# A recurrent attention and an MLP on one core: a new order of emission, placed by the program's scheduler instead of by hand

## The chip, the cores and the metric

The kernel runs on one core of a Trainium2 chip. The metric is the device time of one execution, in microseconds (us). PE is the matrix engine (TensorE), DVE the vector engine, ACT the scalar engine, POOL GpSimd and SP the engine that issues most transfers. Each engine takes its own instructions in a fixed order and waits, at the head of its queue, for what the next one needs. Differences within some tenths of a per cent are the spread of a single kernel.

## The reference

```python
def _attn_ref(q, k, v, alpha):          # (4, 8, 768, 48)
    for t in range(S):
        state = alpha[:, :, t, :, None] * state + np.einsum('bhd,bhe->bhde', k[:, :, t], v[:, :, t])
        y[:, :, t] = np.einsum('bhd,bhde->bhe', q[:, :, t], state)

def _moe_ref(x, w_in, w_out, g_ln):     # x: the attention's y as (3072, 384)
    h = x @ w_in                        # d_ff 1024
    e = np.exp(h - h_max)
    solu = h * (e / (np.sum(e, axis=-1, keepdims=True) + 1e-09))
    ln = (solu - mu) / np.sqrt(var + 1e-06) * g_ln
    return (ln @ w_out).astype(np.float32)
```

q, k, v and alpha are fp32. The weights and the gains of the norm arrive as float64; the kernel turns the words of the weights into fp32 itself.

## The kernel before

**Attention in groups.** The 768 tokens are cut into G = 6 groups of 128; a group covers all 4 batches and 8 heads at once. Within a group the recurrence is written as a masked product. Alpha is transposed (`alpha_T`, L165), so that tokens run along a row; a backward scan gives `hT` (`scan_back`, L181, three instructions of a third each), and a forward scan, seeded by a reciprocal from `hT`, gives the decays that belong to the queries, in `aT` (`scan_on`, L186). Keys are transposed and multiplied by `hT` (`keys_T`, `keys`), queries by `aT` (`queries_T`, `queries`). In `queries` POOL multiplies the ends of the heads' 48 columns (`qe`), ACT separates them into two halves of a head pair (`apart`), and POOL multiplies the first 32 columns (`qv`). PE forms scores (`scores`, L233, in two halves of four heads), DVE masks them into `sT` (`masked`). PE then reads the state with the queries (`read_state`, four parts) and the values with the scores (`read_values`) into y; ACT copies y as four tiles `xT`, one for each batch. `next_state` multiplies the keys turned back (`keys_back`, `kg`) by the values into kv, and DVE adds kv to `state`, which `decay` has scaled on POOL.

**MLP in blocks.** A block n is 128 tokens of one batch, 24 in all, four to each group. `up(n, half)` makes one half of h on PE, then e on ACT, u on DVE and its square on ACT; `partial(n)` adds up e on POOL and the squares on DVE; `down(n, half)` multiplies u by w_out, its second half also forms the two sums; `finish(n)` takes the sums on DVE, a power on POOL, and scales the output on ACT (`o_sb`), which SP writes out.

**Weights.** `pieces` are six parts of w_in (512 wide) and eight of w_out (384 wide). For each: `fetch` loads the raw words on SP's queue into one of four buffers, `bits` makes two fp32 parts by four DVE operations (L437 to L444), `add` sums them on PE (L457) and copies the sum by ACT, `in_range` runs two ACT operations over the raw words for the final test of the inputs. `centre` subtracts the mean from the eight parts of w_out (L499, L501).

**What sets the order.** `tc.manual_schedule()` is entered right after the pools, so each engine's instructions stand in the order in which the code emits them. The order is written out: a prologue (conversion of three pieces, group 0's attention), then the first four blocks' ups between the conversions, then the first downs with group 1's attention, and then a loop over m = 4 to 24 that does up(m), down(m - 1) and finish(m - 2). There s = m % 4 places the attention of group g = m // 4 + 1:

- s = 0: values loaded, backward scans, keys transposed and multiplied, state scaled
- s = 1: keys turned back, forward scans, queries transposed and multiplied; loads of the next group
- s = 2: first half of the scores between the halves of up(m), second half between the halves of down(m - 1)
- s = 3: state reads around the halves of down(m - 1), values, then the next group's alpha and `next_state`

Most of the attention's tiles (`aT`, `hT`, `kT`, `qv`, `qe`, `kg`, `sT`, `vn`, `state`) have one buffer. h has two banks of PSUM, o two, and the tags a0 to a3 one bank each; scores, keys turned back, y and kv share these.

The function returns a flag; `general_path` runs only where the flag says that the inputs lie outside the range that `fast_path` assumes.

Of the kernel before, what the change touches and what calls it, by code (L numbers as in the profile page):

```python
# [32 lines left out]
def fast_path(ctx, tc, q, k, v, alpha, moe_w_in, moe_w_out, moe_g_ln, out):  # L33
# [104 lines left out]
    def turned(src, out):  # L138

        x = by_token(src)  # L140
        ends = two.tile([P, B, H * E1], FP, tag="two", name="ends")
        nc.scalar.copy(out=ends.rearrange("p b (h d) -> p b h d", h=H), in_=x[:, :, :, E0:D])
        for j in range(NB):
            for b in range(B):
                cols = x[:, b, j, 0:E0] if j < H else ends[:, b, E0 * (j - H) : E0 * (j - H) + E0]
                nc.tensor.matmul(
                    out[j // NP][32 * b : 32 * b + 32, j % NP], lhsT=cols, rhs=ident, start=True, stop=True,
                    tile_position=(0, 32 * b), skip_group_check=True,
                )
# [4 lines left out]
            for dst, src in ((slice(0, E0), slice(0, E0)), (slice(48, 64), slice(E0, D))):  # L154
                nc.sync.dma_start(out=vn[:, b, :, dst], in_=v[b, :, t, src].rearrange("h p d -> p h d"))

    def blocks(src, dst, extra):

        nc.vector.transpose(out=dst.rearrange("p h (t u) -> p h u t", u=TQ), in_=src[:, :, :, 0:E0])  # L159
        nc.vector.transpose(  # L160
            out=extra.rearrange("p j (i t u) -> p u j i t", u=TQ, i=2),
            in_=src[:, :, :, E0:D].rearrange("p (j i) u d -> p u j i d", i=2),
        )

    def alpha_T(g):  # L165
        nc.gpsimd.memset(aT[:, :, 0:1], 0.0)
# [34 lines left out]
            nc.gpsimd.tensor_tensor(out=kT[:, part], in0=kT[:, part], in1=hk[:, part], op=ALU.mult)  # L201

    def queries_T(g):
        blocks(qn, qv[:, 0:H], qe)

    def apart():
        for i in range(2):
            nc.scalar.mul(
                out=qv[:, H : 2 * H].rearrange("p (j i) t -> p j i t", i=2)[:, :, i], in_=qe, mul=parity[:, i : i + 1]
            )  # L210

    def queries(g):
        nc.gpsimd.tensor_tensor(out=qe, in0=qe, in1=aT[:, H:NB, 1:SW], op=ALU.mult)
        apart()
        nc.gpsimd.tensor_tensor(out=qv[:, 0:H], in0=qv[:, 0:H], in1=aT[:, 0:H, 1:SW], op=ALU.mult)  # L215

    def decay(g):
# [208 lines left out]
    far = const.tile([P, len(pieces), 2], FP, name="far")  # L426
    made = {}

    def bits(i):
# [13 lines left out]
        nc.vector.tensor_scalar(out=power, in0=top, scalar1=0xFF800000, scalar2=None, op0=ALU.bitwise_and)  # L443
        nc.vector.scalar_tensor_tensor(out=low, in0=lo, scalar=2.0**-52, in1=low, op0=ALU.mult, op1=ALU.mult)  # L444
        made[i] = low, top.bitcast(FP)

    def add(i):

# [14 lines left out]
    def in_range(i):  # L463


        if not float64:
            return
        F = words(i)[0].shape[1]
        raw = raws.pop(i)
        sq = work.tile([P, 512], FP, name="sq")[:, 0:F]  # L470
        nc.scalar.activation(
            out=sq, in_=raw[:, 0:F, 1].bitcast(FP), func=AF.Square, accum_out=far[:, i, 0:1]
        )
        nc.scalar.activation(out=sq, in_=sq, func=AF.Exp, scale=-(2.0**24), accum_out=far[:, i, 1:2])
# [31 lines left out]
    def inline(x, name):  # L506
        return nc.inline_tensor(np.ascontiguousarray(x, np.float32), name=name).ap()

    nc.scalar.dma_start(out=ident, in_=inline(np.eye(P), "ident_c"))
    for i in range(3):  # L510
        fetch(i)
    load_first(alpha, an)
# [3 lines left out]
    nc.scalar.dma_start(out=g_rows, in_=moe_g_ln.rearrange("(c p) -> c p", p=P))  # L516
    load_first(k, kn)
    load_first(q, qn)
    nc.gpsimd.memset(unit, 0.0)
    nc.gpsimd.memset(unit[:, :, 0:1], 1.0)  # L520
    nc.gpsimd.memset(vn, 0.0)
    nc.gpsimd.memset(aT[:, :, 0:1], 0.0)
    nc.gpsimd.memset(hT[:, NB * SW : NB * SW + 2], 1.0)
    for s in seed:
# [5 lines left out]
    load_v(0)  # L530
    fetch(3)

    for i in range(3):
        bits(i)
        add(i)
    alpha_max(0)
    t = banks("tp_a", [NP, P], 3)
    turned(an, t)
    for i in range(3):
        nc.scalar.copy(out=aT[:, NP * i : NP * i + NP, 1:SW], in_=t[i])  # L540
    for i in range(3):
        in_range(i)
        fetch(i + 4)
        scan_back(0, i)
    t = [ps_h.tile([P, NP, P], FP, tag="h", name=f"tp_k{i}") for i in range(2)]
    t.append(ps_a.tile([P, NP, P], FP, tag="a3", name="tp_k2"))
    turned(kn, t)
# [4 lines left out]
    turned(qn, t)  # L552
    for i in (2, 0, 1):
        scan_on(0, i)
        part = slice(NP * i, NP * i + NP)
# [4 lines left out]
            apart()  # L560
    gains()
    scores(0, 0)
    bits(3)
    masked(0)
    scores(0, 1)
    add(3)
    masked(1)
    bits(4)
    read_begin()
    read_values(0)  # L570
    add(4)
    for i in (3, 4):
        in_range(i)
        fetch(i + 4)
    load(alpha, an, 1)


    up(0, 0)
    up(1, 0)
    bits(5)  # L580
    add(5)
    keys_back(0)
    next_state(0)
    in_range(5)
    fetch(9)
    load(k, kn, 1)
    up(0, 1)
    convert(6)
    fetch(10)
    up(1, 1)  # L590
    partial(0)
    convert(7)
    fetch(11)
    partial(1)
    convert(8)
    fetch(12)
    up(2, 0)
    convert(9)
    fetch(13)
    load(q, qn, 1)  # L600
    load_v(1)
    up(2, 1)
    partial(2)
    convert(10)
    convert(11)
    up(3, 0)
    convert(12)
    convert(13)
    up(3, 1)
    centre()  # L610
    partial(3)
    alpha_T(1)
    alpha_max(1)
    for i in range(3):
        scan_back(1, i)
    decay(1)
    down(0, 0)
    down(0, 1)
    keys_T(1)
    keys(1)  # L620
    finish(0)
    for i in range(3):
        scan_on(1, i)
    down(1, 0)
    down(1, 1)
    queries_T(1)
    queries(1)
    finish(1)
    keys_back(1)
    down(2, 0)  # L630
    down(2, 1)
    scores(1, 0)
    masked(0)
    finish(2)
    scores(1, 1)
    masked(1)
    down(3, 0)
    down(3, 1)
    load(alpha, an, 2)
    load(k, kn, 2)  # L640
    load(q, qn, 2)
    read_begin()
    for i in range(4):
        read_state(i)
    read_values(1)
    alpha_T(2)
    alpha_max(2)
    finish(3)
    next_state(1)
    for m in range(B, N + 1):  # L650
        g, s = m // B + 1, m % B
        attn, more = m < N and g < G, g + 1 < G
        rise, fall = m < N, m > B
        if attn and s == 0:
            load_v(g)
        if rise:
            up(m, 0)
# [7 lines left out]
        if m > B + 1:  # L665
            finish(m - 2)
        if attn and s == 3:
            read_begin()
            read_state(0)
            read_state(1)  # L670
        if fall:
            down(m - 1, 0)
        if attn and s == 2:
            scores(g, 1)
            masked(1)
        if attn and s == 3:
            read_state(2)
            read_state(3)
        if fall:
            down(m - 1, 1)  # L680
        if not attn:
            continue
        if s == 0:
            for i in range(3):
                scan_back(g, i)
            keys_T(g)
            decay(g)
            keys(g)
        elif s == 1:
            keys_back(g)  # L690
            for i in range(3):
                scan_on(g, i)
            queries_T(g)
            queries(g)
# [489 lines left out]
```

## Time and profile before

| | |
|---|---|
| median of 3 runs | 556.03 us (553.51 to 556.2) |
| the profiled execution, its own time | 554.89 us |
| its span in the profile | 553.0 us |
| mean clock granted to PE in it | 0.883 |
| read from and written to HBM | 25.30 MB and 4.72 MB, mean 56 GB/s |

The span runs from the first to the last instruction; 1.9 us of the execution lie outside it. Where a row of a view gives a wait, it is the idle time of that engine just before the instruction and the engine and line that ended it. "issue" is time for which the profile shows no releaser.

### The profile page before, as it was taken

How to read it: one execution, taken by the hardware profiler on the slowest of the kernel's cores; microseconds unless marked ns; L12 is line 12 of the kernel's file. 1: busy time of each engine (PE TensorE's matmuls, PEld its weight loads, DVE VectorE, ACT ScalarE, POOL GpSimd, SP SyncE). 2: the span in 40 equal slices, each digit the busy share in tenths (PEclk: the TensorE clock that was granted, in tenths of full speed). 3: DMA queues.
4: the chain of work that ended last, by engine and by line, in shares of the span. 5: the costliest groups of instructions: out<-in, count | busy, mean ns of one | idle time of the engine just before them, and what ended most of it. 6: DMA issues, size and time to landing. Idle time of an engine off the chain costs nothing.

```text
span 553.0 us, 12123 instructions
## 1 busy us (share of the span) xinstructions
PE 435.9 (79%) x5365; PEld 345.1 (62%) x5365; DVE 273.3 (49%) x483; ACT 130.5 (24%) x252; POOL 140.6 (25%) x148
## 2 busy tenths in 40 slices
PE   4769755478669598389995699994899948999993
PEld 1558543345447496367884577884589736888772
DVE  4583335444973338444477245583542873313431
ACT  1603423233020032111222212231122221223220
POOL 3000021201420026222064302362220832202430
PEclk9878887879886899579998789996899988999997
DMA  6970441530003564012235130415213100000001
GB/s 161 177 160 6 113 112 57 99 45 0 0 30 78 110 101 88 0 32 43 41 48 107 22 72 19 58 32 112 58 32 44 31 15 0 17 18 15 14 17 49
DMA packets 85118, 30.90 MB, mean 56 GB/s; under 512 B 64568, under 2 KB 83264, under 8 KB 85056
## 3 DMA queue, kind: packets, MB, share of 16 engines
q1 hardware_dynamic: 84608, 29.90, 26.4%
q8 instruction: 44, 0.72, 0.6%
q10 hardware_dynamic: 448, 0.14, 0.1%
q14 instruction: 18, 0.15, 0.1%
HBM read 25.30 MB, written 4.72 MB: 54 GB/s over the span
## 4 chain that ended last, share of the span: by engine, by line
PE 55%; DVE 28%; issue 5%; ACT 5%; POOL 3%; DMA 2%; SPq 0%; DVEq 0%; ACTq 0%
PE h L329 18%; PE o L358 11%; PE a L239 8%; PE y L271 8%; PE sum L457 6%; DVE aT L179 3%; DVE hT L179 3%; DVE u L335 2%; DVE part_u L344 2%; DVE part_u L347 2%; ACT e L334 2%; ACT u L336 2%; DVE qv L159 2%; DVE kT L159 2%; DVE sT L250 2%
## 5 line engine op out<-in xcount | busy, mean ns | idle before, releaser
L329 PE MATMUL h<-xT,w_in 128*128 128x128 f32 x1152 | 138.4, 280 | 0.0
L329 PEld LDWEIGHTS h<-xT,w_in 128*128 128x128 f32 x1152 | 134.9, 196 | 5.1 <-issue 4.1
L358 PE MATMUL o<-w_out,u 128*128 128x385 f32 x384 | 134.5, 500 | 1.1 <-DVE w_out L501 0.6
L335 DVE TENSOR_TENSOR u<-h,e 128x512 f32<-128x512 f32 x48 | 33.2, 691 | 170.4 <-ACT e L334 170.4
L344 POOL TENSOR_TENSOR part_e<-e 128x512 f32<-128x512 f32 x24 | 30.6, 1273 | 292.3 <-ACT e L334 292.3
L358 PEld LDWEIGHTS o<-w_out,u 128*128 128x128 f32 x384 | 72.0, 194 | 49.0 <-issue 4.9
L239 PE MATMUL a<-qv,kT 32*128 32x128 f32 x768 | 51.6, 396 | 55.5 <-POOL qv L215 34.1
L239 PEld LDWEIGHTS a<-qv,kT 32*128 32x128 f32 x768 | 46.0, 294 | 61.8 <-POOL qv L215 34.8
L334 ACT ACTIVATE e<-h 128x512 f32<-128x512 f32 x48 | 28.5, 593 | 102.7 <-PE h L329 102.6
L457 PE MATMUL sum<-low,ident 128*128 128x384 f32 (+1 forms) x28 | 21.3, 858 | 35.4 <-DVE low L444 35.4
L336 ACT ACTIVATE u<-u 128x512 f32<-128x512 f32 x48 | 30.2, 630 | 48.7 <-DVE u L335 48.7
L250 DVE TENSOR_TENSOR sT<-a,mask 128x512 f32<-128x512 f32 x48 | 29.7, 680 | 21.3 <-PE a L239 21.3
L386 ACT ACTIVATE o_sb<-o,r 128x384 f32<-128x384 f32 x24 | 14.0, 582 | 109.7 <-POOL r L384 109.7
L457 PEld LDWEIGHTS sum<-low,ident 128*128 128x128 f32 x28 | 6.3, 265 | 41.1 <-DVE low L444 23.3
L384 POOL TENSOR_TENSOR r<-sums,mhalf 128x1 f32<-128x1 f32 x24 | 15.8, 660 | 54.7 <-DVE sums L380 54.6
L347 POOL TENSOR_TENSOR part_e<-part_e 128x256 f32<-128x256 f32 x24 | 28.3, 1181 | 1.9
L344 DVE TENSOR_TENSOR part_u<-u 128x512 f32<-128x512 f32 x24 | 19.0, 793 | 14.6 <-ACT u L336 14.6
L271 PE MATMUL y<-sT,vn 128*32 128x128 f32 x768 | 24.4, 290 | 0.0
L271 PE MATMUL y<-qv,state 32*32 32x128 f32 x1280 | 19.1, 281 | 5.8 <-issue 5.8
L271 PEld LDWEIGHTS y<-sT,vn 128*32 128x32 f32 x768 | 22.5, 118 | 1.5 <-issue 1.1
L296 ACT COPY xT<-y 128x384 f32<-128x384 f32 x24 | 11.5, 479 | 46.6 <-PE y L271 46.6
L179 DVE TENSOR_TENSOR_SCAN aT<-aT,seed 128x516 f32<-128x516 f32 x18 | 22.2, 1232 | 0.6
(101 smaller groups left out, 437.7 us busy)
## 6 DMA issues: line engine op xcount, KB each, us to landing
an<-in_alpha_dram SPq DMA_DIRECT2D x24, 192.0 KB, 4.1
kn<-in_k_dram SPq DMA_DIRECT2D x24, 192.0 KB, 5.0
qn<-in_q_dram SPq DMA_DIRECT2D x24, 192.0 KB, 4.5
out_dram<-o_sb SPq DMA_DIRECT2D x24, 192.0 KB, 1.9
vn<-in_v_dram SPq DMA_DIRECT2D x24, 128.0 KB, 3.4
raw<-in_moe_w_out_dram SPq DMA_DIRECT2D x8, 384.0 KB, 3.9
raw<-in_moe_w_in_dram SPq DMA_DIRECT2D x16, 128.0 KB, 3.2
vn<-in_v_dram SPq DMA_DIRECT2D x24, 64.0 KB, 3.1
```

Of the source, the lines that this page charges most:

```text
L179: nc.vector.tensor_tensor_scan(out=o, data0=a, data1=s, initial=1.0, op0=ALU.mult, op1=ALU.add)
L239: nc.tensor.matmul(a[b][:, i], lhsT=kT[quarter(b), kb], rhs=qv[quarter(b), qb], start=kb == h, stop=kb != h, tile_position=(32 * b, 0), sk ...
L250: nc.vector.tensor_tensor(out=sT[:, b, half * NP : half * NP + NP], in0=a[b], in1=mask[:, None, :].to_broadcast([P, NP, P]), op=ALU.mult,)
L271: nc.tensor.matmul(reading["y"][b][quarter(r), a], lhsT=lhsT, rhs=rhs, start=(b, r) not in begun, stop=stop, tile_position=(row, 32 * r), ...
L329: nc.tensor.matmul(h[:, f], lhsT=w_in[:, a, (f0 + f) * P : (f0 + f + 1) * P], rhs=d["xT"][:, a], start=(a == 0), stop=(a == KC - 1),)
L334: nc.scalar.activation(out=d["e"][:, fs], in_=h, func=AF.Exp)
L335: nc.vector.tensor_tensor(out=d["u"][:, fs], in0=h, in1=d["e"][:, fs], op=ALU.mult)
L336: nc.scalar.activation(out=d["u2"][:, fs], in_=d["u"][:, fs], func=AF.Square)
L344: eng.tensor_tensor(out=t, in0=d[key][:, 0:HF], in1=d[key][:, HF:FC], op=ALU.add)
L347: eng.tensor_tensor(out=t[:, 0:w], in0=t[:, 0:w], in1=t[:, w : 2 * w], op=ALU.add)
L358: nc.tensor.matmul(o[:, 0 : DM + 1], lhsT=d["u"][:, f], rhs=w_out[:, f], start=(f == 0), stop=(f == FC - 1), skip_group_check=True,)
L457: nc.tensor.matmul(src, lhsT=ident, rhs=x, start=k == 0, stop=k == 1)
```

## The change

The line that enters the manual order is gone. The program's scheduler now places each engine's instructions: it ranks them by the order of emission and takes ahead what it holds ready. The order of emission is drawn up anew as well. The work itself is the same; the core of the diff:

```diff
-    ctx.enter_context(tc.manual_schedule())
...
-    def blocks(src, dst, extra):
+    def blocks(src, dst, extra, flip=False):
...
+        for o, i in both[::-1] if flip else both:
+            nc.vector.transpose(out=o, in_=i)
...
     def queries(g):
         nc.gpsimd.tensor_tensor(out=qe, in0=qe, in1=aT[:, H:NB, 1:SW], op=ALU.mult)
-        apart()
         nc.gpsimd.tensor_tensor(out=qv[:, 0:H], in0=qv[:, 0:H], in1=aT[:, 0:H, 1:SW], op=ALU.mult)
...
         made[i] = low, top.bitcast(FP)
+        in_range(i)
...
-    def convert(i):
-        bits(i)
-        add(i)
-        in_range(i)
...
+    up(0, 0)
+    add(3)
+    bits(5)
+    fetch(9)
+    up(1, 0)
     add(4)
...
+    up(0, 1)
+    bits(7)
+    fetch(11)
+    add(6)
+    partial(0)
+    up(1, 1)
+    add(7)
+    bits(8)
...
         if rise:
             up(m, 0)
-        if attn and s == 2:
-            scores(g, 0)
+        if attn and s == 0:
+            load_v(g)
+            scan_back(g, 0)
+            scan_back(g, 1)
+        elif attn and s == 1:
+            scan_on(g, 2)
+            queries_T(g)
+            queries(g)
         if rise:
             up(m, 1)
             partial(m)
-        if attn and s == 2:
+        if attn and s == 1:
+            apart()
+        elif attn and s == 2:
+            scores(g, 0)
             masked(0)
...
         if fall:
             down(m - 1, 0)
-        if attn and s == 2:
-            scores(g, 1)
-            masked(1)
...
         elif s == 2:
+            scores(g, 1)
+            masked(1)
             if more:
                 load(q, qn, g + 1)
```

In the prologue alpha is loaded ahead of the weights, the copy of the heads' ends (`ends_of`) is emitted apart from the transposes (`turned`), and the sums of the first pieces stand between the transposes of alpha, keys and queries. After the conversions group 1's scans, keys and queries are emitted further ahead: keys before the first down, queries before the second.

What that does to the engines' rows is shown at three places. The first is DVE at the end of the conversion, before:

```order
L335 TENSOR_TENSOR u<-h,e 128x512
L437 TENSOR_SCALAR top<-raw 128x384
L440 SCALAR_TENSOR_TENSOR top<-raw,top 128x384
L443 TENSOR_SCALAR low<-top 128x384
L444 SCALAR_TENSOR_TENSOR low<-raw,low 128x384
L335 TENSOR_TENSOR u<-h,e 128x512
L501 TENSOR_TENSOR w_out<-w_out,mean 128x384 x8
L344 TENSOR_TENSOR part_u_1023<-u_938 128x512
L347 TENSOR_TENSOR part_u_1023<-part_u_1023 128x256
L349 TENSOR_TENSOR sum_u_1024<-part_u_1023 128x128
L159 STREAM_TRANSPOSE aT<-an 128x8x4x32
L160 STREAM_TRANSPOSE aT<-an 128x4x4x32
```

and in the changed kernel, where L454 to L461 are the four word operations, L339 is u and L184 a scan:

```order
L339 TENSOR_TENSOR u<-h,e 128x512
L353 TENSOR_TENSOR sum_u_922<-part_u_921 128x128
L454 TENSOR_SCALAR top<-raw 128x384
L184 SCALAR_TENSOR_TENSOR hT<-aT,unit 128x516
L457 SCALAR_TENSOR_TENSOR top<-raw,top 128x384
L184 SCALAR_TENSOR_TENSOR hT<-aT,unit 128x516
L460 TENSOR_SCALAR low<-top 128x384
L454 TENSOR_SCALAR top<-raw 128x384
L461 SCALAR_TENSOR_TENSOR low<-raw,low 128x384
L457 SCALAR_TENSOR_TENSOR top<-raw,top 128x384
L339 TENSOR_TENSOR u<-h,e 128x512
```

Group 1's alpha has been transposed and is scanned between the word operations of the last pieces; before, all of that stands behind the centring of w_out.

The second place is DVE in the loop, where a group's state is updated. Before (L159 and L160 transpose, L317 adds kv, L335 is u of the next block, L344 to L349 are its partial sums):

```order
L159 STREAM_TRANSPOSE aT<-an 128x8x4x32
L160 STREAM_TRANSPOSE aT<-an 128x4x4x32
L170 TENSOR_REDUCE amax<-an 128x1
L317 TENSOR_TENSOR state<-state,kv_2790 128x8x64
L317 TENSOR_TENSOR state<-state,kv_2791 128x8x64
L335 TENSOR_TENSOR u<-h,e 128x512 x2
L344 TENSOR_TENSOR part_u_2890<-u_2852 128x512
L347 TENSOR_TENSOR part_u_2890<-part_u_2890 128x256
```

In the changed kernel (L168 transposes, L377 to L384 are a block's sums, L321 adds kv, L184 scans):

```order
L168 STREAM_TRANSPOSE qv<-qn 128x8x4x32
L168 STREAM_TRANSPOSE aT<-an 128x8x4x32
L377 COPY sums<-o 128x3
L379 TENSOR_TENSOR sq<-sums 128x2
L381 SCALAR_TENSOR_TENSOR t<-sq,sums 128x1
L384 SCALAR_TENSOR_TENSOR sums<-sq,t 128x1
L321 TENSOR_TENSOR state<-state,kv_2111 128x8x64
L321 TENSOR_TENSOR state<-state,kv_2112 128x8x64
L184 SCALAR_TENSOR_TENSOR hT<-aT,unit 128x516 x3
L194 COPY fend<-hT 128x4
L197 TENSOR_SCALAR least<-hT 128x4
```

A later group's query transpose and scans have moved up to the state's update; before, the scans stand behind the next block's u and partial sums, and the query transpose a block later still.

The third place is ACT at the end of a group, where y is copied. Before:

```order
L334 ACTIVATE e<-h 128x512
L336 ACTIVATE u_2517<-u 128x512
L386 ACTIVATE o_sb<-o,r 128x384
L296 COPY xT<-y_2571 128x384
L296 COPY xT<-y_2572 128x384
L296 COPY xT<-y_2573 128x384
L296 COPY xT<-y_2574 128x384
```

and in the changed kernel, with L213 the two pieces of the queries' ends:

```order
L338 ACTIVATE e<-h 128x512
L340 ACTIVATE u_2515<-u 128x512
L213 ACTIVATE qv<-qe,parity 128x4x128 x2
L390 ACTIVATE o_sb<-o,r 128x384
L300 COPY xT<-y_2558 128x384
L300 COPY xT<-y_2559 128x384
L300 COPY xT<-y_2560 128x384
L300 COPY xT<-y_2561 128x384
```

The next group's two pieces have moved ahead of this group's copies of y. On PE the score products keep their alternation over the four banks; each half of the scores now stands behind a whole up or a whole down.

More of the change, by code (lines that the diff above doesn't have):

```diff
@@ L203, in queries_T @@
     def queries_T(g):
-        blocks(qn, qv[:, 0:H], qe)
+        blocks(qn, qv[:, 0:H], qe, True)
     def apart():
@@ L427, in fast_path, with in_range @@
     made = {}
+    def in_range(i):
+        if not float64:
+            return
+        F = words(i)[0].shape[1]
+        raw = raws.pop(i)
+        sq = work.tile([P, 512], FP, name="sq")[:, 0:F]
+        nc.scalar.activation(
+            out=sq, in_=raw[:, 0:F, 1].bitcast(FP), func=AF.Square, accum_out=far[:, i, 0:1]
+        )
+        nc.scalar.activation(out=sq, in_=sq, func=AF.Exp, scale=-(2.0**24), accum_out=far[:, i, 1:2])
     def bits(i):
@@ L507, in inline @@
         return nc.inline_tensor(np.ascontiguousarray(x, np.float32), name=name).ap()
+    load_first(alpha, an)
     nc.scalar.dma_start(out=ident, in_=inline(np.eye(P), "ident_c"))
-    for i in range(3):
-        fetch(i)
-    load_first(alpha, an)
     nc.scalar.dma_start(out=mask, in_=inline(np.triu(np.ones((P, P))), "mask_c"))
@@ L529, in fast_path @@
     nc.vector.memset(w_out[:, :, DM : DM + 1], 1.0)
[L530 to L535, printed above, removed]
+    t = banks("tp_a", [NP, P], 3)
+    turned(an, ends_of(an), t)
     alpha_max(0)
-    t = banks("tp_a", [NP, P], 3)
-    turned(an, t)
     for i in range(3):
         nc.scalar.copy(out=aT[:, NP * i : NP * i + NP, 1:SW], in_=t[i])
+    bits(0)
+    ends = ends_of(kn)
     for i in range(3):
-        in_range(i)
-        fetch(i + 4)
         scan_back(0, i)
+    add(0)
     t = [ps_h.tile([P, NP, P], FP, tag="h", name=f"tp_k{i}") for i in range(2)]
     t.append(ps_a.tile([P, NP, P], FP, tag="a3", name="tp_k2"))
-    turned(kn, t)
+    turned(kn, ends, t)
+    fetch(4)
+    bits(1)
+    fetch(5)
+    ends = ends_of(qn)
     for i in range(3):
@@ L551, in fast_path @@
     t = banks("tp_q", [NP, P], 3)
-    turned(qn, t)
+    turned(qn, ends, t)
+    add(1)
     for i in (2, 0, 1):
@@ L602, in fast_path @@
     up(2, 1)
+    add(9)
+    bits(11)
     partial(2)
-    convert(10)
-    convert(11)
     up(3, 0)
-    convert(12)
-    convert(13)
+    add(10)
+    bits(12)
+    add(11)
+    bits(13)
     up(3, 1)
+    add(12)
+    add(13)
     centre()
@@ L615, in fast_path @@
         scan_back(1, i)
+    keys_T(1)
+    keys(1)
     decay(1)
@@ L618, in fast_path @@
     down(0, 1)
-    keys_T(1)
-    keys(1)
-    finish(0)
+    load(alpha, an, 2)
     for i in range(3):
         scan_on(1, i)
+    finish(0)
+    queries_T(1)
+    queries(1)
     down(1, 0)
     down(1, 1)
-    queries_T(1)
-    queries(1)
     finish(1)
-    keys_back(1)
+    apart()
+    load(k, kn, 2)
     down(2, 0)
     down(2, 1)
+    keys_back(1)
+    finish(2)
+    down(3, 0)
     scores(1, 0)
     masked(0)
-    finish(2)
+    load(q, qn, 2)
+    down(3, 1)
     scores(1, 1)
     masked(1)
[L637 to L641, printed above, removed]
+    finish(3)
     read_begin()
@@ L683, in fast_path @@
         if s == 0:
-            for i in range(3):
-                scan_back(g, i)
+            scan_back(g, 2)
             keys_T(g)
+            keys(g)
             decay(g)
-            keys(g)
+            scan_on(g, 0)
+            scan_on(g, 1)
         elif s == 1:
             keys_back(g)
[L691 to L694, printed above, removed]
             if more:
```

91 lines of the change are left out of this document (41 added, 50 removed).

## The prediction

> **What bounds the kernel now.** I read the page's busy totals first, then the chain that ended last, then busy time by stage, then the waits in the stages that lose most.
>
> ```profile
> span 553.0 us, 12123 instructions
> PE 435.9 (79%) x5365; PEld 345.1 (62%) x5365; DVE 273.3 (49%) x483; ACT 130.5 (24%) x252; POOL 140.6 (25%) x148
> ...
> PE 55%; DVE 28%; issue 5%; ACT 5%; POOL 3%; DMA 2%; SPq 0%; DVEq 0%; ACTq 0%
> ```
>
> PE is busy for 435.9 of 553.0 us, yet only 55% of the chain is PE's; 28% is DVE's. So PE is the engine with most to do, and elsewhere it stands behind DVE. No other engine comes near half the span. The question is where the 117 us of PE's idle time lie. The columns are the stretch, its length, each engine's busy time, PE's clock and the DMA share:
>
> ```profile
> 50.00:138.00 88.00, 59.18 (x395) 41.38 (x388) 34.66 (x65) 31.52 (x76) 11.05 (x13) 0.84 0.32 68
> 138.00:164.00 26.00, 16.07 (x60) 10.71 (x59) 24.28 (x32) 2.47 (x5) 10.76 (x9) 0.87 0.02 8
> 164.00:198.00 34.00, 27.20 (x629) 23.01 (x630) 11.30 (x20) 4.46 (x10) 1.17 (x3) 0.75 0.41 83
> 198.00:272.50 74.50, 60.59 (x873) 51.05 (x873) 39.21 (x60) 15.45 (x27) 22.79 (x22) 0.86 0.27 52
> 272.50:347.20 74.70, 64.29 (x893) 52.57 (x893) 40.31 (x68) 16.62 (x29) 24.72 (x24) 0.91 0.28 54
> 347.20:422.20 75.00, 64.57 (x897) 52.77 (x893) 40.35 (x68) 16.62 (x29) 24.73 (x24) 0.91 0.28 54
> 422.20:493.80 71.60, 61.18 (x797) 50.00 (x797) 35.14 (x64) 16.13 (x28) 24.66 (x23) 0.93 0.13 23
> 493.80:553.00 59.20, 50.02 (x294) 39.00 (x294) 17.93 (x53) 13.78 (x23) 15.61 (x18) 0.94 0.06 23
> ```
>
> From 50 to 138 us (the weights are converted beside the first blocks) PE works 59.2 of 88 us and DVE 34.7: neither is full, so they take turns. From 138 to 164 DVE is full (24.28 of 26) and PE waits for it. From 198 on, a group of four blocks takes about 74.7 us and leaves PE about 10.4 idle, at a clock of 0.91.
>
> **The conversion stage.** A piece of the chain there:
>
> ```profile
> 99.15 2.76 PE sum L457 x4
> 101.91 3.13 PE h L329 x24
> ...
> 110.39 0.57 DVE low L444
> ...
> 111.09 5.43 PE sum L457 x8
> ...
> 132.26 0.93 PE mean L499 x2
> ```
>
> And the wait by itself, in the list of waits (total, times, longest):
>
> ```profile
> PE sum L457 <- DVE low L444: 35.4, 8, 8.3
> ```
>
> PE sums a piece of weight, makes one half of h, then stands from 105.04 to 111.09 while ACT and DVE finish with h and DVE only afterwards makes the next piece's words; then PE works and DVE stands. The change emits each piece's four word operations one step ahead of its sum and of the half of h, and in the new order DVE also does group 1's preparation between them. That is this work, now between 138 and 156:
>
> ```profile
> 138.40 1.93 DVE aT L159
> ...
> 142.71 3.46 DVE hT L179 x3
> 146.18 1.90 DVE kT L159
> ...
> 152.08 1.23 DVE aT L179
> ```
>
> 1.93 for alpha, 3.46 for the three backward scans, 1.90 for the keys, 3 x 1.23 = 3.7 for the forward scans: 11.0 of large operations. With the smaller ones between them and the waits for POOL it takes some 16.5 of the 17.0 us from 138.40 to 155.4. Up to the first down product, DVE then has 34.7 + 16.5 = 51.2 us and PE 59.2, side by side. I start at 50.6, where the values of group 0 end on both orders (what comes earlier there has the same transposes and scans behind the same loads; I give it nothing, with 3 us either way). Followed row by row, with these durations, the coupling of the two costs about 4 us over PE's 59.2, so the first down product begins at 50.6 + 63.1 = 113.7, against 133.8 now (the mean's product ends at 133.2). From there to the end of the state reads PE has four downs (22), keys turned back (1.5), scores (4.5 warm) and state reads (3.7), 31.7, and I take 6 of waits (masks, centring): 151.5. The values and kv (5.5) and one wait of 2.1 (below) put the end of kv at **159.1 instead of 198, a gain of 38.9**. It can't exceed 45.5: from 50 to 198 PE has 102.5 busy of 148. If the word operations and u still block each other in DVE's order, half the first gain (10) is lost. Part of the gain is a stall that I let go:
>
> ```profile
> 183.74 5.82 issue
> ```
>
> Nothing in the trace releases PE there; it falls at the end of the burst of loads of all three inputs, which the new order spreads over the downs.
>
> The page "Runtime: NRT & Kernel Launch" of the Trainium skill, section "Instruction fetch mechanics", says that an engine's instructions are fetched in blocks over its own DMA queue, and that crossing a block is mostly hidden. The row of 5.82 us with no releaser beside a loaded DMA would be an exception, if it is a fetch; by the rule the sum is as I have it, by the row it could come back in a group, which is a rival below.
>
> **The steady groups.** The wait for scores, PE's rows of the group from 272.5:
>
> ```profile
> 294.40 1.51 PE L258 MATMUL tp<-ident,kT 128*128 128x128 f32 x12
> ...
> 306.34 3.79 PE L239 MATMUL a<-qv,kT 32*128 32x128 f32 x64 [7.75 <-POOL qv L215]
> ...
> 318.22 3.03 PE L239 MATMUL a<-qv,kT 32*128 32x128 f32 x39 [2.22 <-DVE sT L250]
> ```
>
> PE stands 7.75 us for the queries and 2.22 for the masks that free the banks. Behind the first wait lies a chain of DVE and POOL:
>
> ```profile
> 300.05 1.95 DVE qv L159
> ...
> 304.16 2.14 POOL qv L215
> ...
> 322.72 3.73 PE o L358 x8
> ...
> 332.25 1.83 PE y L271 x102
> 334.08 2.79 PE o L358 x8
> ...
> 341.83 3.63 PE y L271 x128
> 345.46 1.77 PE kv L308 x96
> ...
> 469.96 2.02 PE a L239 x58
> ...
> 504.86 5.47 PE h L329 x48
> 510.33 5.19 PE o L358 x16
> 515.52 0.34 PE o L364 x4
> ```
>
> In the changed order the backward scans and alpha's transposes for the next group stand right behind the state's update, and the transposes of the queries, their POOL products and ACT's two pieces stand a block ahead of the scores: the 6.3 us of this chain (300.05 to 306.30) then lie under ups and downs, and the 7.75 go. The first half of the scores now stands behind a whole up, not between its halves. Behind that up DVE does u, the partial sums and the four masks (4 x 0.68 in the page's groups); PE has scores (2.2), a whole down and its sums (5.5) in that time, 7.7 against some 6.6: the 2.22 go too. What remains is PE's work at full clock. One block's up, down and sums take 5.47 + 5.19 + 0.34 = 11.0, four 44.0; the state reads 2 x 1.83, values 3.63 and kv 1.77 add 9.1; scores are two times 2.02 x 64/58 = 4.5, and the turned keys 1.5: **59.1**. The same rows show what a wait does to the clock: eight products of a down took 3.73 behind the two waits and 2.79 later.
>
> The page "TensorE: Matmul & The Clock Gate" of the Trainium skill, section "Part 1: The HAM clock gate", has two speeds, the slow one after an idle window of some 3.4 us. The 7.75 us agree (3.73 and 3.79 behind it). By the rule a wait of about 2 us costs itself alone, and the sum would be 4 lower than what I predict.
>
> The added cost: on DVE the next group's query transpose (1.95) waits for the last state read, since it rewrites qv; queued behind it are alpha's transpose and a block's sums, for which POOL's power and ACT's scaling wait. On ACT the next group's two query pieces and that scaling stand ahead of the four copies of xT; kv's two banks are those that the first two copies free, and the next up needs all four. From the page's groups:
>
> ```profile
> L250 DVE TENSOR_TENSOR sT<-a,mask 128x512 f32<-128x512 f32 x48 | 29.7, 680 | 21.3 <-PE a L239 21.3
> ...
> L386 ACT ACTIVATE o_sb<-o,r 128x384 f32<-128x384 f32 x24 | 14.0, 582 | 109.7 <-POOL r L384 109.7
> ...
> L384 POOL TENSOR_TENSOR r<-sums,mhalf 128x1 f32<-128x1 f32 x24 | 15.8, 660 | 54.7 <-DVE sums L380 54.6
> ...
> L296 ACT COPY xT<-y 128x384 f32<-128x384 f32 x24 | 11.5, 479 | 46.6 <-PE y L271 46.6
> ```
>
> From the last state read that is 1.95 + 1.93 on DVE, some 0.6 for the sums, 0.66 on POOL, 0.58 for the scaling and 2 x 0.48 for two copies, 6.7, and about 2.2 more of handovers and of the wait for POOL's product that frees aT: 8.9. PE has half a down, its sums and the values in that time, 2.79 + 0.34 + 3.63 = 6.8. So kv waits **2.1**. The trace has no such wait: before, the copies end with the values. It lies between 0 and the 7.75 of the nearest chain, and 2.1 stands near the 2.22 of the other wait on a DVE step. The order of score tiles on PE is kept, so their overlap is too.
>
> So a group with kv comes to 59.1 + 2.1 + 0.5 of small waits = 61.7, the last one without kv and its wait 57.7. Group 2 has one down less (5.5), but its first block's u now stands behind the hoisted scans, which holds the second slot of h: 5.8 by the rows of three scans and their small operations; 61.5 in all. Gains: group 2 **74.5 - 61.5 = 13.0**, then **74.7 - 61.7 = 13.0**, **75.0 - 61.7 = 13.3**, **71.6 - 57.7 = 13.9**. The tail from 493.8 (59.2, PE 50.02) has the same order: nothing. The manual order itself has no instruction; loads and the range checks are moved, not added, and ACT (24%) and the queues have room: nothing. On SP's queue a piece's load waits for the range check that frees its buffer; the check now stands right behind the piece's words on ACT, so the buffer comes free no later than before; if one is late, it costs up to the 8.3 of the longest wait for words, once, in the range.
>
> **Sum.** 38.9 + 13.0 + 13.0 + 13.3 + 13.9 = 92.1. The span goes from 553.0 to 460.9; with the 1.9 around it (the profiled execution took 554.89) 462.8. I add 4 for a clock that falls at the waits before kv, 0.94 a time by the two rows of the down (3.73 - 2.79), four times: **466.8**. The median shown, 556.03, is 1.1 above the profiled execution, which changes nothing.
>
> **Rivals.**
> - *Part of it is turned into new waits.* The wait before kv is as long as today's chain (7.75 instead of 2.1, four times: +22.6), or the 5.82 stall returns in each group (+23), and the conversion keeps half of its turns (+10): about 495. For it: the copies of xT stand behind three engines. Against it: each of those was done long before in the rows I followed.
> - *Better.* No wait before kv (8.4) and none at group 2's first block (5.8), no loss of clock (4): about 449.
> - *Slower.* One mechanism: the early pieces of the next group's queries on ACT hold the xT copies for the whole preparation, because it is not done when the values end. The preparation is 11.0 of large DVE operations, with the queries' chain (6.3) 17.3, and a cold clock behind it costs 0.94 for each half of a down, some 4 in all: 21. PE would lose 19 more than I have in each of five groups: 467 + 95 = 562. From 18 us a group it is slower than now. Against: it would have to start only when the values end, and DVE is busy 40.31 of 74.70 us.
> - *No difference, or the change doesn't do what it says.* The new order of rows shows that it does; no change needs gains and losses of 90 us that cancel.
> - The rule on fetching and that on the clock give 466.8 and 462.8, inside my own case.
>
> **Chances.** Forecast (450 to 485) 0.61; partly eaten (485 to 520) 0.21; better than 450 0.09; slower 0.06; about the same 0.02; the rest lies between 520 and 553. The range that holds eight in ten, leaving out the best few and the worst of the partly eaten ones, is 446 to 506. A difference of 0.5% (2.8 us) is about what a measurement of this kernel can tell from none. Faster 0.92, same 0.02, slower 0.06.
>
> **What would show it.** PE's wait for qv before the scores is gone, and the wait for masks; windows of a group near 62 us with 59 to 61 busy at a clock near 0.95; the first down near 114; PE's waits for word operations (35.4 in the list of waits) mostly gone; kv waits near 2 us for ACT. Wrong if PE waits at kv or at the first up of a group for over 6 us, if DVE is full between 50 and 114 while PE stands, or if stalls without a releaser appear in the reads.

## The result and the profile after

The changed kernel takes **455.5 us** (median of 4 runs, 453.8 to 457.57) beside 555.68: a ratio of 0.8205, 95% interval 0.816 to 0.825. The forecast was 466.8 in a range of 446 to 506. The profiled execution took 453.8, its span is 452.0. The page's totals and its chain:

```profile
span 452.0 us, 12096 instructions
PE 407.2 (90%) x5365; PEld 321.4 (71%) x5365; DVE 270.2 (60%) x483; ACT 129.6 (29%) x252; POOL 139.0 (31%) x148
...
PE 67%; DVE 17%; SPq 6%; issue 3%; POOL 2%; DMA 2%; ACT 1%; DVEq 0%
```

DVE, ACT and POOL do what they did before. PE has the same 5365 products, but they take 28.7 us less (435.9 before): the mean granted clock is 0.960 instead of 0.883. The other 72 us are PE's idle time. By stage, each window ending with PE's last kv product of a group (columns as before):

```profile
0.00:46.46 46.46, 31.57 (x557) 22.80 (x557) 26.94 (x50) 13.49 (x28) 5.18 (x13) 0.93 0.74 148
46.46:110.54 64.08, 51.05 (x379) 37.61 (x375) 50.36 (x85) 32.97 (x79) 18.69 (x18) 0.89 0.49 105
110.54:156.96 46.42, 43.46 (x688) 30.95 (x688) 37.57 (x60) 7.03 (x12) 12.40 (x11) 0.89 0.38 87
156.96:216.44 59.48, 55.60 (x873) 46.31 (x873) 39.90 (x64) 15.64 (x28) 23.59 (x23) 1.00 0.37 74
216.44:277.27 60.83, 59.26 (x896) 48.77 (x893) 40.06 (x69) 16.22 (x29) 23.47 (x24) 1.00 0.33 67
277.27:336.33 59.06, 59.06 (x897) 48.85 (x893) 36.61 (x66) 16.22 (x29) 24.02 (x23) 1.00 0.17 33
336.33:393.61 57.28, 57.28 (x800) 47.06 (x796) 21.46 (x45) 14.84 (x26) 16.65 (x19) 1.00 0.15 29
393.61:452.00 58.39, 49.95 (x298) 39.02 (x294) 17.32 (x45) 13.20 (x22) 15.01 (x17) 0.95 0.06 20
```

From 277 to 393 PE does not stand at all. Group 4, of 59.06 us, is PE's own work, the 59.1 of the prediction. PE's instructions, with the wait ahead of each:

```profile
96.76 1.62 PE L475 MATMUL sum<-low,ident 128*128 128x384 f32 x2 [3.93 <-DVE low L461]
...
110.54 7.14 PE L362 MATMUL o<-w_out,u 128*128 128x385 f32 x16 [2.56 <-DVE w_out L501]
...
138.01 5.20 PE L243 MATMUL a<-qv,kT 32*128 32x128 f32 x64 [0.90 <-DVE sT L254]
...
154.21 0.95 PE L275 MATMUL y<-sT,vn 128*32 128x128 f32 x25 [1.09 <-issue]
...
164.58 2.94 PE L333 MATMUL h<-xT,w_in 128*128 128x128 f32 x24 [1.69 <-DVE u L339]
...
190.69 3.48 PE L243 MATMUL a<-qv,kT 32*128 32x128 f32 x64
...
214.54 1.97 PE L312 MATMUL kv<-vn,kg 128*32 128x64 f32 x96 [1.60 <-ACT xT L300]
...
245.24 2.07 PE L243 MATMUL a<-qv,kT 32*128 32x128 f32 x64
...
252.96 2.07 PE L243 MATMUL a<-qv,kT 32*128 32x128 f32 x64
...
275.37 1.97 PE L312 MATMUL kv<-vn,kg 128*32 128x64 f32 x96 [1.57 <-ACT xT L300]
...
334.45 1.95 PE L312 MATMUL kv<-vn,kg 128*32 128x64 f32 x96
```

In group 3 both halves of the scores (245.24 and 252.96) stand without a wait and take 2.07 us each, where the first took 3.79 behind 7.75 of waiting. In group 2 the second half (190.69) still takes 3.48: within the row PE's weight loads wait for masks, at a granted clock of 1.00. The new waits are 1.6 us ahead of kv, twice.

### The profile page after: what moved, and what is told of

Same layout as the page of the kernel before. It is cut to its first block, busy times and chain, and to the rows that moved or that the text cites. A ratio compares the mean times of both kernels' runs of the same rounds, so it can differ in the third digit from the quotient of the medians.

```text
span 452.0 us, 12096 instructions
## 1 busy us (share of the span) xinstructions
PE 407.2 (90%) x5365; PEld 321.4 (71%) x5365; DVE 270.2 (60%) x483; ACT 129.6 (29%) x252; POOL 139.0 (31%) x148
## 4 chain that ended last, share of the span: by engine, by line
PE 67%; DVE 17%; SPq 6%; issue 3%; POOL 2%; DMA 2%; ACT 1%; DVEq 0%
PE h L333 25%; PE o L362 24%; PE y L275 7%; PE a L243 4%; PE sum L475 3%; DVE aT L168 3%; SPq L134 2%; SPq L425 2%; DVE aT L184 2%; PE kv L312 2%; DVE hT L184 2%; SPq L156 2%; PE tp L262 2%; DVE sT L254 1%; PE o L368 1%
## 5 line engine op out<-in xcount | busy, mean ns | idle before, releaser
L333 PEld LDWEIGHTS h<-xT,w_in 128*128 128x128 f32 x1152 | 132.9, 193 | 6.9 <-DVE u L339 2.4
L362 PE MATMUL o<-w_out,u 128*128 128x385 f32 x384 | 132.7, 496 | 2.6 <-DVE w_out L501 2.6
L339 DVE TENSOR_TENSOR u<-h,e 128x512 f32<-128x512 f32 x48 | 32.9, 686 | 76.5 <-ACT e L338 76.5
L388 POOL TENSOR_TENSOR r<-sums,mhalf 128x1 f32<-128x1 f32 x24 | 13.2, 551 | 75.1 <-DVE sums L384 75.1
L243 PE MATMUL a<-qv,kT 32*128 32x128 f32 x768 | 31.6, 289 | 2.7 <-DVE sT L254 1.7
L475 PE MATMUL sum<-low,ident 128*128 128x384 f32 (+1 forms) x28 | 15.7, 649 | 19.6 <-DVE low L461 18.9
L243 PEld LDWEIGHTS a<-qv,kT 32*128 32x128 f32 x768 | 28.0, 196 | 5.4 <-DVE sT L254 3.2
L184 DVE TENSOR_TENSOR_SCAN hT<-aT,unit 128x516 f32<-128x516 f32 x18 | 23.6, 1347 | 1.5 <-ACT aT L538 0.8
L206 POOL TENSOR_TENSOR kT<-kT,hT 128x1024 f32<-128x1024 f32 (+1 forms) x10 | 16.9, 1703 | 19.5 <-DVE kT L168 19.5
L377 DVE COPY sums<-o 128x3 f32<-128x3 f32 x24 | 3.8, 159 | 30.8 <-PE o L368 30.8
L275 PE MATMUL y<-qv,state 32*32 32x128 f32 x1280 | 21.4, 294 | 0.7 <-DVE sT L254 0.6
```

Source lines behind the costliest of these rows:

```text
L184: nc.vector.tensor_tensor_scan(out=o, data0=a, data1=s, initial=1.0, op0=ALU.mult, op1=ALU.add)
L243: nc.tensor.matmul(a[b][:, i], lhsT=kT[quarter(b), kb], rhs=qv[quarter(b), qb], start=kb == h, stop=kb != h, tile_position=(32 * b, 0), sk ...
L275: nc.tensor.matmul(reading["y"][b][quarter(r), a], lhsT=lhsT, rhs=rhs, start=(b, r) not in begun, stop=stop, tile_position=(row, 32 * r), ...
L333: nc.tensor.matmul(h[:, f], lhsT=w_in[:, a, (f0 + f) * P : (f0 + f + 1) * P], rhs=d["xT"][:, a], start=(a == 0), stop=(a == KC - 1),)
L339: nc.vector.tensor_tensor(out=d["u"][:, fs], in0=h, in1=d["e"][:, fs], op=ALU.mult)
L362: nc.tensor.matmul(o[:, 0 : DM + 1], lhsT=d["u"][:, f], rhs=w_out[:, f], start=(f == 0), stop=(f == FC - 1), skip_group_check=True,)
```

## The experiments

The theory: PE's idle time was the order of DVE's and ACT's queues, and only that. Open was what had mended it, the new order of emission or the scheduler, and whether the small waits had the causes that were named. Each ratio is to the kernel before on the same chip.

**e1: the old order of emission, left to the scheduler.**

```diff
-    ctx.enter_context(tc.manual_schedule())
```

> The order of emission of before, with the line for the manual order taken out and nothing else. Theory 1 (the scheduler's look-ahead empties DVE's queue early, whatever order it is given): PE's wait for qv (7.75 us a group) is gone, the words of a piece stand ahead of its sum, and only the waits for masks stay, since the halves of the scores are where they were; 470 us, between 460 and 480. Theory 2 (the new order of emission does it, the scheduler keeps close to the rank it is given): above 530 us.

455.44 us, ratio 0.8222 (0.8188 to 0.8257). That is the changed kernel's ratio within the intervals. The scheduler alone does it; the new order of emission, on top of it, gives nothing that can be measured in the time. In the loop PE's waits are nearly those of the changed kernel too, down to the two ahead of kv (total, times, longest):

```profile
PE kv L306 <- ACT xT L294: 3.2, 2, 1.6
```

Ahead of the loop they differ: PE waits 11.1 us for words instead of 18.9, but 6.2 for w_out and once 5.9 for masks, and kv(1) ends 1.5 us later, which the time does not show. My 470 for it was too high: the wait for masks went from the loop as well, although on PE the halves of the scores stand where the old order has them.

**e2: the new order, by hand.**

```diff
     ps_a = pool("ps_a", 1, space=PS)
+    ctx.enter_context(tc.manual_schedule())
```

> The changed kernel with the line for the manual order put back, so the new order of emission stands as written. Theory 1 (order and scheduler each suffice for the loop): groups of 59 to 61 us and no wait before kv, but group 1's preparation (16.5 us) stands behind the centring again, so the first scores come 5 to 10 us later; 455 to 465 us. Theory 2 (the scheduler does it): above 500 us.

470.61 us, 0.849 (0.8455 to 0.8526): 15 us of the 100 are missing, and not where I had put them, since the first scores of group 1 come at 129.10, ahead of the scheduled kernel's 131.92. The conversion is shorter by hand: the mean's product, which the scheduled kernel reaches at 106.30, comes at 91.31. That lead is given back, and 15 us more, in two places, PE's rows:

```profile
91.31 0.91 PE L501 MATMUL mean<-quarters,ones 128*128 128x384 f32 x2 [0.64 <-ACT quarters L499]
...
118.02 6.85 PE L364 MATMUL o<-w_out,u 128*128 128x385 f32 x16 [13.73 <-ACT o_sb L392]
...
243.75 4.66 PE L245 MATMUL a<-qv,kT 32*128 32x128 f32 x64 [4.08 <-ACT kg L266]
```

The third down waits 13.73 us for a bank that block 0's output still holds. Its sums stand on DVE behind group 1's scans:

```profile
114.85 1.23 DVE L186 TENSOR_TENSOR_SCAN aT<-aT,seed 128x516 f32<-128x516 f32 x1
116.00 0.13 DVE L379 COPY sums<-o 128x3 f32<-128x3 f32 x1
```

And in three groups the scores wait for ACT to copy the keys turned back, which stands behind a scaling that itself waits for POOL:

```profile
242.55 0.58 ACT L392 ACTIVATE o_sb<-o,r 128x384 f32<-128x384 f32 x1 [4.00 <-POOL r L390]
243.03 1.55 ACT L266 COPY kg<-tp 128x512 f32<-128x512 f32 x3
```

**e3 and e4: the halves of the new order, by hand.** e3 is the kernel before with only the new loop over m; e4 is e2 with the old loop.

The loop's part of the diff, of which these are some lines, is in e3 and not in e4:

```diff
-        if attn and s == 2:
-            scores(g, 0)
...
+        elif attn and s == 1:
+            scan_on(g, 2)
+            queries_T(g)
+            queries(g)
...
         elif s == 2:
+            scores(g, 1)
+            masked(1)
```

> The kernel before, by hand, with only the loop over m in its new order. By the sum of the prediction the groups give 13.0 + 13.0 + 13.3 + 13.9 = 53.2 us, up to 57 if no wait before kv takes their place: 499 to 503 us. If the groups and the conversion were not independent (work pushed from one into the other), it is above 515.

> The new order of emission by hand, with the loop over m as before: the conversion and group 1 alone. By the sum of the prediction 38.9 us less than before, less the 5 to 10 that the scheduler's early preparation of group 1 is worth: 517 to 527 us. If the conversion only gains through the scheduler, above 540.

e3: 515.95 us, 0.9312 (0.9271 to 0.9353). e4: 507.45 us, 0.915 (0.9106 to 0.9193). Both missed: the loop by hand gave 37, not 53, and what is missing is mostly the waits for kg (12.2 us in three groups of e3) and the scores behind them (4.4 to 4.7 us where 2.07 would do); the first part gave 46, not 29 to 39. The two add up (37.4 + 45.9 = 83.3) to what e2 gave, 82.7, so by hand loop and first part do not feed each other.

**e5: the first finish ahead of group 1's scans (on e2).**

```diff
+    alpha_T(1)
+    down(0, 0)
+    down(0, 1)
+    finish(0)
     alpha_max(1)
...
     for i in range(3):
         scan_on(1, i)
-    finish(0)
```

> The new order by hand (470.6 us), with the first down and its finish emitted ahead of group 1's scans. Theory: PE's 13.7 us before the third down are DVE's order alone, since the sums of the first block stand behind the scans; the wait goes. But group 1's scores still need the same chain on DVE, 0.7 longer by the sums, so PE is late there instead: 5 to 8 of the 13.7 are won, 463 to 466 us. Rival (ACT or the output's transfer held the bank): the wait stays, 470.

469.42 us, 0.8466 (0.8421 to 0.8512): about 1 us, within the intervals of the two. The third down no longer waits, so DVE's order was the cause; but the fourth now does, for the second block's output behind the same scans:

```profile
123.53 4.66 PE L364 MATMUL o<-w_out,u 128*128 128x385 f32 x8 [11.44 <-ACT o_sb L392]
```

I had moved one block's sums and left the next where they were.

**e6: keys turned back ahead of a block's finish (on e2).**

```diff
         if attn and s == 1:
+            keys_back(g)
             apart()
...
         elif s == 1:
-            keys_back(g)
```

> The new order by hand (470.6 us), with the keys turned back ahead of a block's finish in the loop, so that ACT copies them before it waits to scale an output. Theory: the 4.1 us for kg before the first scores of three groups go, with the cold products behind them (4.66 for 2.07, 6.55 for 5.45): 3 x 6 to 7.8, 447 to 453 us. Rival (the copies are late because u is late on DVE): another wait takes the place, above 460.

464.22 us, 0.84 (0.8345 to 0.8454). The waits for kg are gone, which settles their cause, but other waits stand in their place: in each of three groups 1.53 us for o_sb ahead of a down and 0.61 for masks, with scores of up to 5.39 us behind, and in group 2 once 4.30 for POOL's keys. Groups 3 and 4 take 65 us, and the time is the rival's, above 460.

**e7: group 1 laid out anew, by hand (with e6).**

```diff
+    alpha_T(1)
     up(0, 1)
...
+    for i in range(3):
+        scan_back(1, i)
     centre()
     partial(3)
...
+    down(0, 0)
+    down(0, 1)
+    finish(0)
     for i in range(3):
-        scan_back(1, i)
+        scan_on(1, i)
     keys_T(1)
     keys(1)
...
```

> By hand: the new order with the keys of e6, and group 1 laid out anew: alpha transposed ahead of the second halves, backward scans while DVE waits for the mean, the first finish ahead of the forward scans, keys before queries. Theory (what the scheduler gave over the old order was only a place for DVE's work in gaps, and a place by hand in the right gaps gives at least as much): end of kv(1) near 133 instead of 149.9, groups of 60 to 61: 434 to 442 us. Rival (the conversion has no gap that is free of cost, as in the scheduled kernel, whose mean comes at 106.3 instead of 91.3): 450 to 456.

454.42 us, 0.8196 (0.8157 to 0.8235). Group 1's kv ends at 140.25 instead of 156.96: a place by hand in DVE's real gaps costs the conversion nothing (the mean at 90.94, in e2 at 91.31). The groups from 3 on lose it again, at 65 us against 59 to 61 of the scheduled kernel:

```profile
103.00:140.25 37.25, 31.06 (x668) 23.11 (x666) 24.05 (x30) 6.43 (x12) 10.52 (x11) 0.91 0.39 82
140.25:200.76 60.51, 56.21 (x873) 47.27 (x873) 43.11 (x60) 15.24 (x27) 23.70 (x22) 0.94 0.32 61
200.76:266.00 65.24, 62.53 (x893) 51.30 (x893) 44.56 (x68) 16.41 (x29) 25.73 (x24) 0.97 0.32 62
```

What they lose it to are the waits of e6, PE's rows of group 3:

```profile
233.64 5.45 PE L364 MATMUL o<-w_out,u 128*128 128x385 f32 x16 [1.53 <-ACT o_sb L392]
...
240.03 4.93 PE L245 MATMUL a<-qv,kT 32*128 32x128 f32 x64 [0.60 <-DVE sT L256]
```

**e8: the loads for group 2 spread, in the kernel before.**

```diff
-    load(alpha, an, 2)
-    load(k, kn, 2)
-    load(q, qn, 2)
     read_begin()
```

(the three now stand ahead of group 1's forward scans, behind the second finish, and behind the first masks)

> The kernel before, with the three loads for group 2 issued one after the other between the downs, as in the changed kernel, instead of all at once ahead of the state reads. Theory (the stall of 5.82 us without a releaser comes from the burst of loads): it goes or shrinks below 2, 548 to 551 us beside 553.3. Rival (it falls wherever PE has run that many instructions, whatever the loads do): it stays, and the time is within 0.3%.

548.08 us, 0.9885 (0.9833 to 0.9937). Of the 5.82 us without a releaser, 1.26 are left in that place on the chain:

```profile
183.88 1.26 issue
```

So the burst of loads sets the length of the stall; e3, which keeps the burst, still has 5.58 us there. Its place stays, as the rival had it: the 28 last state reads stand behind it in both kernels. Where two stalls without a releaser follow one another in group 1's reads and values (e1, e2, e4, e5, e7 and e9 to e12), they stand 128 products apart, each product with one weight load. That would fit the fetch of instructions in blocks that the prediction names; what PE waits for there the profile does not say, and no run shows it.

**e9: e7 up to group 1, then the scheduler.** The loads for group 2 are spread as well.

```diff
+    by_hand = tc.manual_schedule()
+    by_hand.__enter__()
     load_first(alpha, an)
...
+    by_hand.__exit__(None, None, None)
     for m in range(B, N + 1):
```

> Up to group 1's kv by hand as in e7 (with the loads for group 2 spread, so that none runs beside the state reads), and the loop left to the scheduler in the changed order. Theory (hand and scheduler each win their stage and the two add up): kv(1) ends near 137 to 140 as in e7, then the groups of the changed kernel, 59.5 + 60.8 + 59.1 + 57.3, and 58.4 behind: 433 to 438 us. Rival (the scheduler's groups are short because it had pushed their preparation into the longer prologue): groups of 62 to 65, above 445 us.

442.52 us, 0.7982 (0.7954 to 0.8011), 13 us below the changed kernel, 4.5 to 9.5 above the forecast. Group 1's kv ends at 141.2, and the group after it takes 64.7 us, the 62 to 65 of the rival; the next two take 60.9 and 59.1. Waits where the two parts meet made the difference; PE's rows:

```profile
126.17 0.91 PE L275 MATMUL y<-qv,state 32*32 32x128 f32 x4 [2.55 <-DVE sT L254]
...
149.97 7.25 PE L333 MATMUL h<-xT,w_in 128*128 128x128 f32 x48 [2.89 <-DVE u L339]
...
203.99 1.97 PE L312 MATMUL kv<-vn,kg 128*32 128x64 f32 x96 [3.40 <-ACT xT L300]
```

The scheduler takes a later group's key transpose ahead between the masks, and its scans ahead of u.

**e10: a block's sums ahead of a later group's alpha (on the changed kernel).** One kind of edge more for the scheduler, on alpha's transposes of groups 3 to 5:

```diff
-            nc.vector.transpose(out=o, in_=i)
+            turn = nc.vector.transpose(out=o, in_=i)
+            if after is not None:
+                tc.add_manual_dep(
+                    turn.ins, after.ins.name,
+                    mybir.DependencyInfo(mybir.DependencyClass.NoSync, mybir.DependencyReason.DATA),
+                    reason="sums first",
+                )
...
-        blocks(an, aT[:, 0:H, 1:SW], aT[:, H:NB, 1:SW])
+        blocks(an, aT[:, 0:H, 1:SW], aT[:, H:NB, 1:SW], after=last_sum.get(B * (g - 3) + 2))
```

> The changed kernel with one more edge in its schedule: alpha's transposes of a later group stand behind the sums of the block whose output ACT scales ahead of the copies of xT. Theory (kv's wait comes from those transposes, as the prediction said): PE's two waits of 1.60 and 1.57 us before kv go, 2 to 3.5 us less, ratio to the changed kernel 0.993 to 0.996. Rival (the chain of POOL and ACT is late for another reason, or a later u is late instead): waits or time unchanged within 0.2%.

449.96 us, 0.814 (0.8101 to 0.818), that is 0.992 of the changed kernel's ratio; the two intervals overlap, the trace is clearer. Both waits ahead of kv are gone, and groups 2 and 3 take 56.8 and 59.1 us instead of 59.5 and 60.8; in the chain (start, length) kv follows the values:

```profile
207.28 3.63 PE y L283 x128
210.91 1.77 PE kv L320 x96
```

**e11: e9 with e10's edge, for groups 4 and 5.**

> e9 (by hand up to group 1, then the scheduler) with the edge of e10. Theory (the waits before kv are one mechanism, wherever the prologue comes from): e9's 5.0 us of waits before kv go, 437 to 439 us, ratio to before near 0.790. Rival (the late u or masks take their place): 441 to 443.

**437.67 us, 0.791 (0.7889 to 0.793)**: as forecast, and the fastest of all, below both kernels. PE's 5.0 us ahead of kv in e9 have shrunk to 0.20.

**e12: e11 with the keys' transposes behind the last mask.**

```diff
-        blocks(kn, kT[:, 0:H], kT[:, H:NB])
+        blocks(kn, kT[:, 0:H], kT[:, H:NB], after=last_mask.get(0) if g > 1 else None)
...
```

> e11 with the transposes of a group's keys placed behind the last mask of the group before, so that the scheduler's early work no longer stands between masks. Theory (what the scheduler takes ahead of masks costs PE there, 2.55 before the state reads of group 1 and 0.77 before scores of group 2, with cold products behind): 2 to 5 us less than e11. Rival (DVE is full there, and the transposes are then late for the next group): the same as e11 within 0.3%.

441.45 us, 0.7969 (0.7945 to 0.7993): 3.8 us slower than e11, against my forecast. The wait for masks ahead of the state reads fell from 2.55 to 0.85, and kv(1) ends 2.7 us earlier. But the work that was held back is done later, ahead of u, and group 2 takes 69.0 us instead of 61.6: e11's row, then e12's.

```profile
149.35 7.25 PE L342 MATMUL h<-xT,w_in 128*128 128x128 f32 x48 [2.78 <-DVE u L348]
```

```profile
125.00 0.91 PE L284 MATMUL y<-qv,state 32*32 32x128 f32 x4 [0.85 <-DVE sT L263]
...
151.74 7.58 PE L342 MATMUL h<-xT,w_in 128*128 128x128 f32 x48 [6.75 <-DVE u L348]
```

## Why the prediction was right, step by step

- **The start.** Group 0's values end at 46.46, not 50.6. I had given the prologue nothing, with 3 us either way; it gave 4.1, a little more than I had allowed.
- **The conversion.** The size was right only by two errors that cancel, which is luck. The first down starts at 110.54 (113.7), 64.08 behind the start (63.1). But I had put PE's work at 59.2 and the coupling at 4; it was 51.05, at a clock of 0.89 instead of 0.84, and 13.0 of waits. A product of the low words took 0.65 us in the mean instead of 0.86, and PE still waits for words, 18.9 us in all, 8.7 of them ahead of the very first sum, before this stage:

```profile
L475 PE MATMUL sum<-low,ident 128*128 128x384 f32 (+1 forms) x28 | 15.7, 649 | 19.6 <-DVE low L461 18.9
```

  Group 1's preparation between the words is not free, as "side by side" has it: DVE is busy for 50.36 of 64.08 us there, and for 24.93 of the 25 us from 85 to 110. e7 and e9, which put part of it into gaps by hand, reach the mean some 15 us earlier. The ceiling of 45.5 on the gain up to kv(1) does not hold either: it took PE's busy time as fixed. From the end of group 0's values to kv(1) PE was busy for 101.8 us before, is for 94.5 here and for 85.7 in e7, whose stretch is 50.1 us shorter than before.
- **The attribution.** "The change emits each piece's four word operations one step ahead" is true of the code, and by hand (e4) that order is worth 46 us with the rest of the first part. But it is not what makes the changed kernel fast: e1 has the old order and the same time.
- **Group 1.** kv ends at 156.96 (159.1). Of the stall of 5.82 us, 1.09 is left, ahead of the last values (154.21), and e8 showed that the burst of loads had made it long.
- **The loop.** The waits for qv went, and those for the masks but for group 2's second half, and PE's own work is 59.1, as worked out from single rows. This carried the forecast.
- **The wait ahead of kv.** 2.1 forecast, 1.60 and 1.57 measured. Its cause was as described: POOL's product frees aT, alpha's transpose follows, and the sums stand behind it on DVE:

```profile
205.80 2.04 DVE L168 STREAM_TRANSPOSE qv<-qn 128x1024 f32<-128x1024 f32 x1 [1.33 <-PE y L275]
210.14 2.12 DVE L168 STREAM_TRANSPOSE aT<-an 128x1024 f32<-128x1024 f32 x1 [2.31 <-POOL qv L219]
212.08 0.19 DVE L377 COPY sums<-o 128x3 f32<-128x3 f32 x1
```

  e10 took this order away, and the wait with it. What I missed: the transpose belongs to the group after next, so group 4 has none left, and its kv (334.45) does not wait.
- **Group 2's first block.** 5.8 forecast for u behind the scans, 1.69 + 0.32 measured: mis-sized.
- **The clock.** The 4 us added for it were not spent. Behind the waits ahead of kv (216.4 to 220.0 and 277.0 to 281.0) the granted clock stays at 1.00. That is what the Trainium skill's "TensorE: Matmul & The Clock Gate", section "Part 1: The HAM clock gate", would have given for a wait well short of its idle window.

Summed, with forecast less measured: 4.1 at the start, -2.0 up to kv(1), 2.0, 0.9, 2.6 and 0.4 in the groups, 0.8 in the tail, 4.0 of clock: 12.9 before rounding, the difference of 464.9 and 452.0. The rivals fell with the rows: no wait in a group of the loop is longer than 1.69, and no stall without a releaser came back in the reads of the loop.

## What to carry to other kernels

Where a chain alternates between engines that are each half idle, ask what is at the head of each queue, and let a scheduler try before an order is rewritten: here it gave the old order all of the gain. Then read where it went too far: it takes work early that fills DVE's queue exactly where PE waits for it, and a region by hand and one kind of extra edge were worth another 18 us (e11). Moving one late instruction mostly uncovers the next one behind the same work (e5, e6, e12).

## What was not expected of the hardware

PE's clock also halved without a long wait. In group 1 PE waits 0.90 us; then the second half of the scores takes 5.20 us where others take 2.07. Some 1.2 of these 5.20 are two more waits for masks, which the row holds (PE's weight loads start anew at 138.61 and 139.21). From 140 to 142 PE is busy without a gap, at a granted clock of 0.50:

```profile
140.00:142.00 2.00, 2.00 (x40) 2.00 (x44) 1.37 (x4) 0.58 (x1) 0.55 (x1) 0.50 0.03 8
```

The page "TensorE: Matmul & The Clock Gate" of the Trainium skill, in the same section, names an idle window of some 3.4 us for that; PE has no wait longer than 0.90 us between 110.54 and this row, so here the rule does not tell the clock. In e7 the scores behind waits of 0.60 us take 4.93 to 5.43 us in three groups, with short waits for masks within the row again and a clock of 0.50 from 243 to 245. What sets the clock was not tried.

A small DVE copy can be held by a long POOL product. Copying `fend`, four values a row, took 1.21 us in the changed kernel while POOL multiplied the keys, and 0.16 in the next group, with POOL at rest. Not every small operation is held: `least`, as small, took 0.16 beside the same product. DVE's rows, then POOL's:

```profile
101.11 1.21 DVE L194 COPY fend<-hT 128x4 f32<-128x4 f32 x1
102.23 0.16 DVE L197 TENSOR_SCALAR least<-hT 128x4 f32<-128x4 f32 x1
102.30 1.15 DVE L194 COPY fend<-hT 128x4 f32<-128x4 f32 x1
...
132.98 0.16 DVE L194 COPY fend<-hT 128x4 f32<-128x4 f32 x1
```

```profile
99.95 3.48 POOL L206 TENSOR_TENSOR kT<-kT,hT 128x1024 f32<-128x1024 f32 x2 [3.75 <-DVE kT L168]
```

The row of POOL holds two products; the first takes 2.34 us alone. The copies end at 102.32 and 103.45, and POOL's products at 102.29 and 103.43: each copy lasts until the product beside it is done. No run moved one of the two to try this.
